# A new eight-visit order for the attention loop of a transformer block on one core

## The chip, the cores and the metric

The kernel runs on one core of a Trainium2 chip. The metric is device time in microseconds (us), from the first to the last instruction of the program, as the median of repeated runs. A core has five engines with a queue of their own each: TensorE (PE; its weight loads are listed as PEld), VectorE (DVE), ScalarE (ACT), GpSimd (POOL) and SyncE (SP, which here only issues DMAs). They meet at semaphores. Products of TensorE land in PSUM, eight banks of 128 x 512 fp32; VectorE or ScalarE read them from there, and a bank can be written again once its reader is done.

## The reference

One transformer block on a sequence of 2048 rows of width 448, all in fp32:

```
h   = x + softmax(q k^T / sqrt(28)) v wo      q = LN(x) wq (16 heads of 28), k, v = LN(x) wk, LN(x) wv (one head for all)
out = h + (silu(LN(h) w1) * (LN(h) w3)) w2    width 1792 inside
```

Softmax is taken over all 2048 keys. No mask.

## The kernel before, in words

**Stages.** Start (LN, queries, keys, values), attention, FFN. The change touches the attention loop.

**Blocks and visits.** Attention runs over 16 blocks `i`: four blocks of 512 query rows times four groups of four heads. Each block has 16 key chunks `c` of 128 keys. A pair (i, c) is a *visit*, 256 in all. A head takes 32 partitions, so that the four heads of a group lie in the four row groups of TensorE, and four products with 32 rows each can run there side by side.

**Head products (`H` in the order, class `Head`).** For each visit and head three products (high and low parts of keys and queries) add up the transposed scores of 128 keys by 512 queries in one bank; after the third ScalarE takes the exponential into a `pt` tile (or into the tiles `xh` and `xl`, which serve as the third buffer). So three `H` tokens of one head give one ScalarE instruction.

**Value products (`pv1`).** For a visit four products with 32 columns each, one per head, add values and the softmax denominator into the bank `po`. After a block's 16 visits ScalarE copies it out to `OT`. The token does nothing when a head of that visit isn't scored yet.

**Score-max units (class `Unit`).** To shift the exponentials, the row maximum of the scores is needed before a block's head products. It comes from separate products in the other orientation: 128 queries by 512 keys per unit, with four query blocks `n`, four key blocks `kt` and four heads, 64 units per block, done some 20 visits ahead. There are several kinds:

- `U`: one product, and VectorE reduces the bank to its maximum (`plain`, L333).
- `D` and `S`: a pair of key blocks a and b. `D` multiplies the query with the difference of the keys a - b (`KD`, made once at the start by GpSimd), and ScalarE evicts the positive part, Relu, to `ab` (L344). `S` multiplies with b, and one VectorE instruction adds `ab` and takes the maximum (L351). max(a, b) = b + Relu(a - b), so VectorE reduces two key blocks with one instruction.
- `E` and `R`: ScalarE copies a bank to the tile `kept` (L358), and VectorE reduces it later from there (L364).

When all 64 units of a block are counted (`counted`), `max_done` and `max_rows` reduce and transpose the maxima (L384, L389), and SP writes them as an extra row into the query tile by four small DMAs (L395).

**The order.** Attention's order is written out: a string `EVERY` of tokens, repeated until the last 20 visits. Before, a cycle has four `pv1`, 48 `H`, 11 `U`, and two `D`, two `S`, one `E` and one `R`. In it, heads 0 and 1 take the first two key blocks of every query block as a pair (`PAIRS`). The tail, a second list, has only head and value products. I call what lies between two value products a *stretch*. All engines run their queue in the order in which the tokens issue.

**Banks.** Seven of the eight banks serve heads and units; `po` has the eighth. `bank()` takes the free one that, by an own small model of the engines (class `Clock`), is free first. The model sets no order; it only decides which earlier eviction a product has to wait for.

Of the kernel before, what the change touches and what calls it, by code (L numbers as in the profile page):

```python
# [8 lines left out]
F32 = mybir.dt.float32  # L9
# [26 lines left out]
def block_kernel(  # L36
# [74 lines left out]
    class Clock:  # L111


        def __init__(self):
            self.mode, self.tile, self.started, self.loaded = None, {}, {}, {}
            self.load = self.start = self.end = self.drained = 0.0
            self.act = self.dve = 0.0

        def mm(self, mode, r, ps, us, first):
            if mode != self.mode:  # L120
                self.mode, self.tile, self.started, self.loaded = mode, {}, {}, {}
                self.drained = self.end + 0.095
            t = max(self.drained, self.load + 0.0035, self.started.get(r, 0.0) + 0.004, self.loaded.get(r, 0.0))
            if first:
                t = max(t, order[used[id(ps)][1]] + 0.017)
            self.load = t
            self.loaded[r] = t + (0.107 if mode != "pv" else 0.025)
            t = max(self.loaded[r], self.tile.get(r, 0.0), self.start + 0.0035)
            self.start = self.started[r] = t
            self.tile[r] = t + us  # L130
            self.end = max(self.end, t + us)
            ready[id(ps)] = t + us + 0.255

        def read(self, eng, t, every):
            t = max(getattr(self, eng), t)
            setattr(self, eng, t + every)
            return t

# [20 lines left out]
    def mm_D(ps0, ps, lhs, rhs, lsl, rsl, between=None, pairs_ab=((0, 0), (1, 0), (0, 1))):  # L159

        terms, rsl_n = [], rsl.stop - rsl.start
        for a, b in pairs_ab:
            terms += [(a, c, b, c) for c in range(3)]
        terms += [(0, 3, 0, 3), (0, 3, 1, 3)]
        for k, (a, ca, b, cb) in enumerate(terms):
            pe.matmul(  # L166
                ps, lhs[b][:, cb, lsl], (rhs[2] if ca == 3 and len(rhs) == 3 else rhs[a])[:, ca, rsl],
                start=(k == 0), stop=(k == len(terms) - 1),
            )
            clock.mm("full", 0, ps0, 0.0182 + rsl_n / 2400, k == 0)  # L170
            if between is not None and k == 5:
                between()
# [83 lines left out]
    def ln_tr_rows(t, n):  # L256
        if n == 0:
            TB.extend(bank() for c in range(4))
        for c in range(4):
            c0 = c * P if c < 3 else D - P  # L260
            pe.transpose(TB[c][:, n * P : (n + 1) * P], LN[t][3][n][:, c0 : c0 + P], ident)
            clock.mm("full", 0, TB[c], 0.109, n == 0)

    def ln_tr(t, c, spare=False):
        ps = last = TB[c] if TB else bank()
        if c == 0:
            XT[t] = xt_tiles()
        c0 = c * P if c < 3 else D - P
        xns = LN[t][3]
        for n in range(NQ):  # L270
            if TB:
                break
            pe.transpose(ps[:, n * P : (n + 1) * P], xns[n][:, c0 : c0 + P], ident)  # L273
            clock.mm("full", 0, ps, 0.109, n == 0)
        to_x(t, c, ps, last, spare)
# [37 lines left out]
    class Unit:  # L313
# [5 lines left out]
        def mm(self, keys=None):  # L319
            i, n, kt, r = self.i, self.n, self.kt, rows(self.j)  # L320
            MX[i] = MXT[i % 2]
            ps = bank("pa")
            pe.matmul(ps, QS[i][r, 0, n * P : (n + 1) * P], KS[0][r, kt * T : (kt + 1) * T] if keys is None else keys[r],  # L323
                      start=True, stop=True)
            clock.mm("rows", self.j, ps, 0.2293, True)
            return ps
# [4 lines left out]
        def red(self):  # L331
            ps = self.ps
            ve.tensor_reduce(self.to(), ps, axis=AX.X, op=ALU.max)  # L333
            done(ps, clock.read("dve", ready[id(ps)], 0.598) + 0.717)

# [4 lines left out]
        def diff(self):  # L340
            ps = self.mm(KDS[self.kt])
            self.ab = ab_pool[n_ab[0] % len(ab_pool)]
            n_ab[0] += 1
            se.activation(self.ab, ps, AF.Relu)  # L344
            t = clock.read("act", ready[id(ps)], 0.477)
            self.t = t + 0.634
            done(ps, t + 0.634)

        def sum(self):
            ps = self.mm(KS[0][:, (self.kt + 1) * T : (self.kt + 2) * T])  # L350
            ve.tensor_tensor_reduce(self.ab, ps, self.ab, 1.0, -3.0e38, ALU.add, ALU.max, self.to())  # L351
            done(ps, clock.read("dve", max(ready[id(ps)], self.t), 0.7) + 0.74)

        def copy(self):
            ps = self.mm()
            self.ab = kept[n_kept[0] % len(kept)]
            n_kept[0] += 1
            se.activation(self.ab, ps, AF.Copy)  # L358
            t = clock.read("act", ready[id(ps)], 0.477)
            self.t = t + 0.634  # L360
            done(ps, t + 0.634)

        def red_copy(self):
            ve.tensor_reduce(self.to(), self.ab, axis=AX.X, op=ALU.max)  # L364
            clock.read("dve", self.t, 0.575)

# [30 lines left out]
    class Head:  # L397
# [5 lines left out]
        def mm(self, k):  # L403
            i, c, r = self.i, self.c, rows(self.j)
            if k == 0:
                self.ps = bank()
            pe.matmul(self.ps, KS[k % 2][r, c * P : (c + 1) * P], QS[i][r, k // 2], start=(k == 0), stop=(k == 2))  # L407
            clock.mm("rows", self.j, self.ps, 0.2293, k == 0)

        def exp(self):  # L410
# [3 lines left out]
            se.activation(f(PT[i, c, p][:, jj]), self.ps, AF.Exp, bias=0.0, scale=SCALE)  # L414
            t = clock.read("act", ready[id(self.ps)], 0.477)
            PR[i, c] = max(PR.get((i, c), 0.0), t + 0.634)
            done(self.ps, t + 0.634)

    def pv(i, c):
        if c == 0:  # L420
            PO[i] = ps_o.tile([P, T], F32, name="po")
        for j in range(4):
            pe.matmul(PO[i][32 * j : 32 * j + 32], VA[:, c], f(PT[i, c, j // 2][:, j % 2]),  # L423
                      start=(c == 0), stop=(c == NC - 1))
        clock.load = max(clock.load, PR.pop((i, c)))
        clock.mm("pv", 0, PO[i], 0.868, False)
        if c == NC - 1:
            g = i % NG
            if i < NI - 2:
                se.activation(OT[:, g], PO.pop(i), AF.Copy)  # L430
            else:
                ve.tensor_copy(OT[:, g], PO.pop(i))
# [65 lines left out]

    PAIRS = (0, 1)
    KD = keep.tile([P, 2, T], F32R, name="KD", tag="q5")  # L500
# [374 lines left out]
    TAIL = LAST - AHEAD  # L875
    heads, left, tail = {}, [0] * 4, False
# [10 lines left out]
    open_d, waiting, later = {}, [], []  # L887
# [8 lines left out]
    kt_ = keep.tile([P, 2, T], F32, name="kept", tag="q4")  # L896
    kept, n_kept = [kt_[:, k] for k in range(2)], [0]

# [12 lines left out]
    def unit(kind, j):  # L911

        if kind == "S":
# [4 lines left out]
            return  # L918
        if kind == "R":
            if waiting:  # L920
                u = waiting.pop(0)
                u.red_copy()
                counted(u.i)
            return
        skip = 4 if kind == "E" else 0
        for k, (_, u, pair) in enumerate(todo_u[j]):
            if pair == (kind == "D"):
                if skip and k + 1 < len(todo_u[j]):
                    skip -= 1
                    continue  # L930
                todo_u[j].pop(k)
                if pair:
                    open_d[j] = u
                    u.diff()
                elif kind == "E":
                    waiting.append(u)
                    u.copy()
                else:
# [26 lines left out]
    while n_pv[0] + LAG < TAIL:  # L965
        for x in EVERY:
            tick()
            if x != "pv1":
# [13 lines left out]

    while waiting:
        unit("R", 0)
    tail = True
    homes, n_qs = [5, 6, 1, 2, 3, 4, 0], [0]
# [34 lines left out]
    def two(pairs):  # L1021
        for units in zip(*pairs):
            for h, (ps, lhs, rhs, first, last) in enumerate(units):
                pe.matmul(ps[:, : rhs.shape[-1]], lhs, rhs, start=bool(first), stop=bool(last), skip_group_check=True)  # L1024
                clock.mm("half", h, ps, 0.016 + rhs.shape[-1] / 2400, first)

# [175 lines left out]
```

## Time and profile before

| what | value |
|---|---|
| median of three runs | 1162.36 us (1159.97 to 1164.62) |
| span of the profiled execution | 1158.6 us |
| granted TensorE clock | 1.000 |
| PE busy | 1149.0 us (99%) |
| VectorE busy | 805.8 us (70%) |
| ScalarE busy | 764.3 us (66%) |
| GpSimd busy | 330.2 us (29%) |
| value products, first to last start | 89.3 to 738.6 us |
| busy within 89.3 to 738.6 us: PE, ScalarE, VectorE | 647.5, 613.7, 552.7 us |

The profile page is of one execution. Its execution has no time on record but its span; the timed runs are others. Busy time counts an engine as busy while any of its instructions is in flight, and instructions overlap in flight, so an engine that is busy all the time may still have room. Matmul ends are modelled. Three stretches of some 9 us within attention, at the end of every fourth block, belong to the output projection.

### The profile page before, as it was taken

The numbers are of one execution on the slowest core, as the hardware profiler recorded it, in microseconds if no ns is written. First come the engines' busy times: TensorE is split into PE (matmuls) and PEld (weight loads), VectorE is DVE, ScalarE is ACT, GpSimd is POOL, SyncE is SP. The second block draws the span as 40 slices with busy tenths as digits, with TensorE's granted clock in tenths as the row PEclk, the third lists the DMA queues.
The fourth block names the chain that finished last, engine by engine and source line by source line (L and its number), as shares of the span: only waits on it lengthen the run. The fifth ranks groups of instructions, "written<-read, shape, count | busy, mean of one in ns | idle before, by whom it ended". The sixth has DMA issues, their size and how long they took to land.

```text
span 1158.6 us, 25640 instructions
## 1 busy us (share of the span) xinstructions
PE 1149.0 (99%) x10154; PEld 772.7 (67%) x10154; DVE 805.8 (70%) x1498; ACT 764.3 (66%) x1587; POOL 330.2 (29%) x242
## 2 busy tenths in 40 slices
PE   8999999999999999999999999999999999999998
PEld 6664444446444445444445444589999999999997
DVE  8878999897999998999988983163543444344333
ACT  5649999997999997999997999512222222222221
POOL 5312001101101111110111011345565556556552
PEclk9999999999999999999999999999999999999999
DMA  4010100001000002000012100143211101000000
GB/s 168 10 38 1 34 13 18 19 15 47 19 12 10 19 24 54 19 20 3 19 24 55 50 19 14 56 103 96 73 39 20 41 1 49 17 33 33 1 1 33
DMA packets 66680, 38.15 MB, mean 33 GB/s; under 512 B 41728, under 2 KB 59392, under 8 KB 66560
## 3 DMA queue, kind: packets, MB, share of 16 engines
q1 hardware_dynamic: 66560, 36.51, 11.5%
q8 instruction: 79, 1.29, 0.5%
q14 instruction: 41, 0.34, 0.1%
HBM read 24.04 MB, written 7.47 MB: 27 GB/s over the span
## 4 chain that ended last, share of the span: by engine, by line
PE 94%; ACT 2%; DVE 2%; issue 1%; DMA 1%; SPq 0%; POOL 0%; ACTq 0%; POOLq 0%
PE po L423 21%; PE pb L407 20%; PE pa L1024 18%; PE pa L323 10%; PE pb L1024 9%; PE pa L166 5%; PE pb L166 4%; PE po L1024 4%; PE pb L1070 1%; ACT OT L430 1%; ACT ab L344 1%; DVE mx L333 1%; PE pb L273 0%; ACT pt L414 0%; PE po L166 0%
## 5 line engine op out<-in xcount | busy, mean ns | idle before, releaser
L333 DVE TENSOR_REDUCE mx<-pa 128x1 f32<-128x512 f32 x689 | 440.1, 685 | 22.1 <-PE pb L407 13.0
L407 PE MATMUL pb<-qs,KS 32*128 32x512 f32 x3072 | 384.9, 425 | 0.0
L414 ACT ACTIVATE pt<-pb 128x512 f32<-128x512 f32 x684 | 365.9, 621 | 20.1 <-PE pb L407 17.3
L407 PEld LDWEIGHTS pb<-qs,KS 32*128 32x128 f32 x3072 | 234.0, 182 | 132.2 <-ACT pt L414 66.9
L323 PE MATMUL pa<-KS,qs 32*128 32x512 f32 x886 | 311.7, 459 | 1.3
L1024 PE MATMUL pa<-xl,qs 64*128 64x512 f32 x1044 | 195.4, 388 | 0.0
L323 PEld LDWEIGHTS pa<-KS,qs 32*128 32x128 f32 x886 | 138.6, 182 | 83.6 <-DVE mx L333 46.3
L423 PE MATMUL po<-pt,VA 128*32 128x512 f32 x1368 | 182.2, 605 | 0.4 <-ACT pt L414 0.4
L1024 PE MATMUL pa<-xh,qs 64*128 64x512 f32 x739 | 159.9, 388 | 0.0
L454 POOL TENSOR_TENSOR OT<-OT,rb 128x512 f32<-128x512 f32 x15 | 19.7, 1311 | 458.1 <-DMA rb<-sd 240.9
L1024 PE MATMUL pb<-w2s,pt 64*128 64x448 f32 x1050 | 145.2, 360 | 0.0
L1034 DVE TENSOR_TENSOR pt<-pa,pt 128x512 f32<-128x512 f32 x49 | 33.8, 691 | 159.0 <-ACT pt L1032 152.9
L1024 PEld LDWEIGHTS pa<-xl,qs 64*128 64x128 f32 x1044 | 141.9, 184 | 3.1
L1024 PEld LDWEIGHTS pb<-w2s,pt 64*128 64x128 f32 x1050 | 125.2, 184 | 2.0 <-DVE pt L1040 0.2
L351 DVE CUSTOM_DVE_ANT_0 ab<-pa,ab 128x512 f32<-128x512 f32 x138 | 93.6, 686 | 39.5 <-PE pa L323 28.4
L1024 PEld LDWEIGHTS pa<-xh,qs 64*128 64x128 f32 x739 | 108.4, 184 | 3.2
L414 ACT ACTIVATE xl<-pb 128x512 f32<-128x512 f32 x170 | 99.6, 610 | 8.9 <-PE pb L407 6.8
L414 ACT ACTIVATE xh<-pb 128x512 f32<-128x512 f32 x170 | 104.5, 633 | 0.0
L1032 ACT ACTIVATE pt<-pa 128x512 f32<-128x512 f32 x49 | 29.3, 597 | 94.7 <-PE pa L1024 90.9
L423 PE MATMUL po<-xl,VA 128*32 128x512 f32 x340 | 89.4, 605 | 0.0
L423 PE MATMUL po<-xh,VA 128*32 128x512 f32 x340 | 89.4, 605 | 0.0
L344 ACT ACTIVATE ab<-pa 128x512 f32<-128x512 f32 x138 | 82.2, 608 | 6.7 <-PE pa L323 4.9
(156 smaller groups left out, 1411.4 us busy)
## 6 DMA issues: line engine op xcount, KB each, us to landing
rb<-sd SPq DMA_DIRECT2D x64, 64.0 KB
xr<-xn SPq DMA_DIRECT2D x64, 56.0 KB
QR<-OT SPq DMA_DIRECT2D x60, 56.0 KB
QR<-in_B_w_dram SPq DMA_DIRECT2D x16, 192.0 KB
xh<-xr SPq DMA_DIRECT2D x4, 768.0 KB
X<-in_A_x_dram SPq DMA_DIRECT2D x3, 896.0 KB
out_dram<-X SPq DMA_DIRECT2D x3, 896.0 KB
w<-in_B_w_dram SPq DMA_DIRECT2D x8, 192.0 KB
```

What stands on the lines that cost most here:

```text
L166: pe.matmul(ps, lhs[b][:, cb, lsl], (rhs[2] if ca == 3 and len(rhs) == 3 else rhs[a])[:, ca, rsl], start=(k == 0), stop=(k == len(terms) - 1),
L323: pe.matmul(ps, QS[i][r, 0, n * P : (n + 1) * P], KS[0][r, kt * T : (kt + 1) * T] if keys is None else keys[r], start=True, stop=True)
L333: ve.tensor_reduce(self.to(), ps, axis=AX.X, op=ALU.max)
L344: se.activation(self.ab, ps, AF.Relu)
L351: ve.tensor_tensor_reduce(self.ab, ps, self.ab, 1.0, -3.0e38, ALU.add, ALU.max, self.to())
L407: pe.matmul(self.ps, KS[k % 2][r, c * P : (c + 1) * P], QS[i][r, k // 2], start=(k == 0), stop=(k == 2))
L414: se.activation(f(PT[i, c, p][:, jj]), self.ps, AF.Exp, bias=0.0, scale=SCALE)
L423: pe.matmul(PO[i][32 * j : 32 * j + 32], VA[:, c], f(PT[i, c, j // 2][:, j % 2]), start=(c == 0), stop=(c == NC - 1))
L454: eng.tensor_tensor(o, o, rb, op=ALU.mult)
L1024: pe.matmul(ps[:, : rhs.shape[-1]], lhs, rhs, start=bool(first), stop=bool(last), skip_group_check=True)
L1032: se.activation(sg, ps[0], AF.Silu)
L1034: ve.tensor_tensor(sg, ps[1], sg, op=ALU.mult)
```

## The change

**The order.** `EVERY` becomes a cycle of eight visits: eight `pv1`, 96 `H`, 22 `U`, five `D` and five `S` tokens. `E`, `R` and their tile `kept` are gone. The loop now stops inside a cycle once the tail is due, and what units are left are then done at once.

**The pairs.** `PAIRS` holds (head, half of the key blocks, parity of the query block): per two query blocks, which are eight visits, head 0 has three pairs and head 1 has two, now also over key blocks 2 and 3. Their difference `KD2` is in both kernels made at the start; it keeps its buffer, which `kept` took over before.

**The tokens' code.** `unit` still keeps one open difference per head in `open_d`; it is not changed but for the loss of `E` and `R`. In the new list the `D` and `S` tokens stand in the order D0 D1 D1 S1 D0 S0 S0 S0 D0 S1. In the built programs:

| instructions | before | changed |
|---|---|---|
| Relu evictions of a difference (ScalarE) | 138 | 167 |
| copies to `kept` (ScalarE) | 59 | 0 |
| sums with maximum (VectorE) | 138 | 80 |
| plain reductions (VectorE) | 689 | 690 |
| reductions of `kept` (VectorE) | 59 | 0 |
| unit products (TensorE) | 1024 | 937 |
| row maxima finished, and transposed (VectorE) | 16 | 1 |
| DMAs of the maxima (SP) | 64 | 4 |

**The clock.** `Clock` gets other constants and rules (load times, read latencies, the value product as four products), which changes the choice of banks throughout.

```
+        LOAD = {"pv": 0.027, "tr": 0.08}
-        def mm(self, mode, r, ps, us, first):
+        def mm(self, mode, r, ps, us, first, after=0.0):
             if mode != self.mode:
-                self.mode, self.tile, self.started, self.loaded = mode, {}, {}, {}
-                self.drained = self.end + 0.095
-            t = max(self.drained, self.load + 0.0035, self.started.get(r, 0.0) + 0.004, self.loaded.get(r, 0.0))
+                self.mode, self.started, self.busy = mode, {}, {}
+                self.load = max(self.load, self.end - 0.075)
+            t = max(self.load + 0.0035, self.started.get(r, 0.0) + 0.002, after)
...
+        def act(self, t):
+            t = max(self.free["act"], t + 0.036, self.last - 0.27)
+            self.free["act"] = t + 0.4767
+            self.last = max(t + 0.592, self.last + 0.49)
+            return self.last
...
-    PAIRS = (0, 1)
+    PAIRS = ((0, 0, 0), (0, 0, 1), (0, 1, 0), (1, 0, 0), (1, 0, 1))
...
-            if j in PAIRS and kt < 2:
-                if kt == 0:
-                    todo_u[j].append((s // NQ, Unit(i, j, n, 0), True))
+            if (j, kt // 2, n % 2) in PAIRS:
+                if kt % 2 == 0:
+                    todo_u[j].append((s // NQ, Unit(i, j, n, kt), True))
...
-    EVERY = "U1 pv1 H3 D0 H1 U2 H3 H0 H1 H3 H0 H1 U2 U3 H0 pv1 D1 H2 S0 H3 H2 U3 H3 H2 H3 H1 H2 H2 H1 H1 U0 H2 H1 H0 H1 H0 U2 H1 H0 U3 pv1 R E3 H0 H2 H1 H0 H3 H2 H1 H3 H2 U0 H3 U2 H0 H1 pv1 H2 H0 S1 H3 H2 U1 H0 H3 H2 H3 H0".split()
+    EVERY = "pv1 D0 H3 H1 H2 H1 H3 H2 U0 H1 H3 U1 H2 U3 pv1 D1 H0 H2 U3 H2 H0 H3 H0 H2 H1 U3 H1 H1 H1 H1 H2 H3 H2 H0 H0 H3 U2 H0 H2 H1 U3 pv1 U2 H1 H0 H3 H3 H1 U2 H0 H3 H0 H1 U2 pv1 D1 H3 H0 H2 U1 H0 H2 H3 H3 H2 S1 H0 pv1 U2 H3 D0 H3 H0 H3 H0 H1 H1 U3 H2 H1 H2 H0 S0 H2 U1 S0 pv1 H1 S0 H3 H2 D0 H1 H3 H2 H0 H1 U2 H0 H3 U1 H2 H0 pv1 U2 H3 H2 H0 H3 H3 H1 H0 H3 H2 H0 H3 H1 H2 U0 H3 H1 U2 pv1 H1 H2 H0 U3 H2 H1 U3 S1 H0 H2 H1 U3 H0".split()
...
     while n_pv[0] + LAG < TAIL:
         for x in EVERY:
+            if n_pv[0] + LAG >= TAIL:
+                break
             tick()
...
-    while waiting:
-        unit("R", 0)
-    tail = True
+    for j in range(4):
+        unit("S", j)
+        while todo_u[j]:
+            for kind in ("DS" if todo_u[j][0][2] else "U"):
+                unit(kind, j)
+    while later:
+        tick()
```

**Where rows move.** First TensorE, in the middle of the loop. The rows go from one value product (`po`) to the next; `pb` are head products, `pa` unit products. Before, one of the two shorter stretches of a cycle:

```order
L423 MATMUL po<-pt,VA 32x512 x4
L323 MATMUL pa<-KS_85,qs 128x512
L407 MATMUL pb<-qs,KS_85 128x512 x3
L407 MATMUL pb<-qs,KS_86 128x512
L407 MATMUL pb<-qs,KS_85 128x512
L407 MATMUL pb<-qs,KS_86 128x512 x3
L407 MATMUL pb<-qs,KS_85 128x512
L323 MATMUL pa<-KS_85,qs 128x512
L407 MATMUL pb<-qs,KS_85 128x512
L323 MATMUL pa<-KS_85,qs 128x512
L407 MATMUL pb<-qs,KS_85 128x512 x2
L423 MATMUL po<-pt,VA 32x512 x4
```

In the changed program, the stretch that has the second `D1`:

```order
L419 MATMUL po<-xh,VA 32x512 x2
L419 MATMUL po<-xl,VA 32x512 x2
L333 MATMUL pa<-KD,qs 128x512
L403 MATMUL pb<-qs,KS_85 128x512 x3
L333 MATMUL pa<-KS_85,qs 128x512
L403 MATMUL pb<-qs,KS_86 128x512 x3
L403 MATMUL pb<-qs,KS_85 128x512 x2
L333 MATMUL pa<-KS_85,qs 128x512
L403 MATMUL pb<-qs,KS_85 128x512
L419 MATMUL po<-pt,VA 32x512 x4
```

Fifteen row products stood in the first, twelve stand in the second: a difference (`KD`), a plain unit, nine head products, and one sum.

Then VectorE, where the maxima of one block end and those of the next begin (`mx_97` and `mx_98` are the two buffers of maxima). Before:

```order
L333 TENSOR_REDUCE mx_97<-pa 128x1
L333 TENSOR_REDUCE mx_98<-pa 128x1 x3
L333 TENSOR_REDUCE mx_97<-pa 128x1
L384 TENSOR_REDUCE neg_82<-mx_97 128x16
L389 STREAM_TRANSPOSE mr<-neg_82 128x32
L351 ISA ab,mx_98<-pa,ab 128x512
L351 ISA mx_98 128x1
L333 TENSOR_REDUCE mx_98<-pa 128x1 x4
L364 TENSOR_REDUCE mx_98<-kept 128x1
```

In the changed program:

```order
L360 ISA ab,mx_97<-pa,ab 128x512
L360 ISA mx_97 128x1
L343 TENSOR_REDUCE mx_97<-pa 128x1 x4
L343 TENSOR_REDUCE mx_98<-pa 128x1
L343 TENSOR_REDUCE mx_97<-pa 128x1 x14
L442 RECIPROCAL sm<-sm 128x16
L343 TENSOR_REDUCE mx_97<-pa 128x1
```

The reduction over a block's maxima (`neg`) and its transpose (`mr`) no longer stand between two blocks, and the reductions form longer runs without a sum between them.

More of the change, by code (lines that the diff above doesn't have):

```diff
@@ L111, in block_kernel @@
     class Clock:
+        LOAD = {"pv": 0.027, "tr": 0.08}
         def __init__(self):
-            self.mode, self.tile, self.started, self.loaded = None, {}, {}, {}
-            self.load = self.start = self.end = self.drained = 0.0
-            self.act = self.dve = 0.0
-        def mm(self, mode, r, ps, us, first):
+            self.mode, self.started, self.busy = None, {}, {}
+            self.load = self.start = self.end = 0.0
+            self.free = {"act": 0.0, "dve": 0.0}
+            self.last = 0.0
@@ L124, in mm @@
             if first:
-                t = max(t, order[used[id(ps)][1]] + 0.017)
+                t = max(t, order[used[id(ps)][1]] + 0.052)
             self.load = t
[L127 to L137, printed above, removed]
+            self.start = t = max(t + self.LOAD.get(mode, 0.105), self.start + 0.0035,
+                                 self.started.get(r, 0.0) + self.busy.get(r, 0.0))
@@ new lines, in mm, with dve @@
+            if mode == "pv":
+                t += us
+            self.started[r], self.busy[r] = t, us
+            ready[id(ps)] = e = t + us + (0.138 if mode == "pv" else 0.158)
+            self.end = max(self.end, e)
+        def act(self, t):
[3 more added lines that the diff above has]
+            return self.last
+        def dve(self, t, every=0.598, lasts=0.685):
+            t = max(self.free["dve"], t + 0.037)
+            self.free["dve"] = t + every
+            return t + lasts
@@ L324, in mm @@
                       start=True, stop=True)
-            clock.mm("rows", self.j, ps, 0.2293, True)
+            clock.mm("rows", self.j, ps, 0.2267, True)
             return ps
@@ L351, in sum @@
             ve.tensor_tensor_reduce(self.ab, ps, self.ab, 1.0, -3.0e38, ALU.add, ALU.max, self.to())
[L352 to L365, printed above, removed]
+            done(ps, clock.dve(max(ready[id(ps)], self.t), 0.6, 0.7))
     def both(i, h, n, kt):
@@ L424, in pv @@
                       start=(c == 0), stop=(c == NC - 1))
-        clock.load = max(clock.load, PR.pop((i, c)))
-        clock.mm("pv", 0, PO[i], 0.868, False)
+        t = PR.pop((i, c)) + 0.051
+        for j in range(4):
+            clock.mm("pv", j, PO[i], 0.4533, False, t)
         if c == NC - 1:
@@ L875, in block_kernel @@
     TAIL = LAST - AHEAD
-    heads, left, tail = {}, [0] * 4, False
+    heads, left = {}, [0] * 4
     todo_u = [[], [], [], []]
@@ L1024, in two @@
                 pe.matmul(ps[:, : rhs.shape[-1]], lhs, rhs, start=bool(first), stop=bool(last), skip_group_check=True)
-                clock.mm("half", h, ps, 0.016 + rhs.shape[-1] / 2400, first)
+                clock.mm("half", h, ps, 0.0133 + rhs.shape[-1] / 2400, first)
     def settle(ps):
```

40 lines of the change are left out of this document (13 added, 27 removed).

## Prediction

> **What bounds the kernel now.** I read the windows first, by stage. The first two quoted windows are eight value visits of the attention loop each, the second of them with a block's end in it; the third is six visits of the tail, where score-max units have run out.
>
> ```profile
> core 0: us, PE busy (x) PEld busy (x) DVE busy (x) ACT busy (x) POOL busy (x), PEclk, DMA share, GB/s
> 296.70:316.30 19.60, 19.60 (x195) 9.51 (x193) 17.80 (x34) 19.29 (x39) 3.13 (x3) 1.00 0.11 27
> 316.30:336.30 20.00, 19.90 (x198) 9.17 (x196) 18.14 (x35) 19.67 (x41) 0.00 (x0) 1.00 0.01 2
> ...
> 711.70:723.70 12.00, 12.00 (x125) 4.79 (x124) 7.87 (x16) 11.96 (x25) 3.35 (x3) 1.00 0.11 30
> ```
>
> TensorE and ScalarE both look full, VectorE nearly so, and the granted clock is 1.00, so no clock effect is involved. Full twice over needs the next view: the chain of waits through one cycle of four visits (start, length, what). `po L423` is the value product, eight records a visit; `pb` and `pa` are head and unit products.
>
> ```profile
> 300.79 1.03 PE po L423 x8
> 301.82 0.42 PE pb L407
> ...
> 302.97 1.00 PE po L423 x8
> ...
> 306.52 1.04 PE po L423 x8
> 307.56 0.43 PE pa L323
> 307.98 0.46 PE pb L407 x8
> ...
> 308.69 0.99 PE po L423 x8
> ...
> 310.64 1.02 PE po L423 x8
> ```
>
> From 300.79 to 310.64 is 9.85 us; the next cycles repeat within 0.05, and two of them are the 19.6 of the window. I use 19.63 for eight visits. The four stretches last 2.18, 3.55, 2.17 and 1.95. On TensorE a stretch costs the value product (1.02), 0.43 until its first row product is through, and then 0.23 for each further *round*: four row products on the four heads' rows run together, and eight took 0.46. Thus TensorE needs 1.22 + 0.23 x rounds, where the rounds are the most products that any one head has in the stretch. Counted from the cycle's list, the stretches have 4, 7, 4 and 3 rounds: 2.14, 2.83, 2.14, 1.91, in all 9.02, or 18.04 per eight visits. Three stretches are at this floor. The long one is not: 3.55 against 2.83. What holds it stands in ScalarE's timeline and in the weight loads that wait within it:
>
> ```profile
> 302.45 0.20 PEld L323 LDWEIGHTS pa<-KS,qs 32*128 32x128 f32 x2 [0.17 <-DVE mx L333]
> 303.90 0.18 PEld L323 LDWEIGHTS pa<-KD,qs 32*128 32x128 f32 x1 [0.84 <-ACT pt L414]
> 305.08 0.18 PEld L323 LDWEIGHTS pa<-KS,qs 32*128 32x128 f32 x1 [0.19 <-ACT ab L344]
> ...
> 302.81 1.57 ACT L414 ACTIVATE pt<-pb 128x512 f32<-128x512 f32 x3
> 304.44 0.60 ACT L344 ACTIVATE ab<-pa 128x512 f32<-128x512 f32 x1
> 304.93 2.06 ACT L414 ACTIVATE pt<-pb 128x512 f32<-128x512 f32 x4
> 306.84 0.64 ACT L414 ACTIVATE xh<-pb 128x512 f32<-128x512 f32 x1
> 307.32 0.65 ACT L414 ACTIVATE pt<-pb 128x512 f32<-128x512 f32 x1
> 308.02 0.60 ACT L358 ACTIVATE kept<-pa 128x512 f32<-128x512 f32 x1
> ```
>
> Four exponentials take 2.06 though one lasts 0.62, so ScalarE starts one every 0.48 when it is fed. From 304.44 to 307.32 it runs at that pace: the long stretch is ScalarE catching up, and TensorE waits in it for the banks that ScalarE (0.19) and VectorE (0.17) still hold. (The 0.84 at 303.90 is the value product itself, which the load has to let pass; it recurs at every visit.) At 306.52 a value product starts; ScalarE has three instructions left, and its next one starts at 308.02, 0.70 after the one before it. Each visit thus costs it a few tenths: 38 instructions in eight visits are 38 x 0.48 = 18.24, and 19.63 - 18.24 = 1.39, or 0.17 per visit. ScalarE bounds the loop, with 0.17 per visit lost because banks and products reach it unevenly. VectorE has 28 reductions, at 0.62 each by the next row ((3.16 - 0.685) / 4), or 17.4: close behind.
>
> ```profile
> span 1158.6 us, 25640 instructions
> ...
> 301.12 3.16 DVE L333 TENSOR_REDUCE mx<-pa 128x1 f32<-128x512 f32 x5
> L333 DVE TENSOR_REDUCE mx<-pa 128x1 f32<-128x512 f32 x689 | 440.1, 685 | 22.1 <-PE pb L407 13.0
> ```
>
> Outside the loop (start to 89 us, FFN after 739 us) the order of the work is unchanged; only bank numbers can move. I cost that at 0, with 2 us either way.
>
> **The change, part by part.** It does not do all that its words say, and that decides the sum. The list opens differences in the order D0 D1 D1 S1 D0 S0 S0 S0 D0 S1, but `open_d` keeps one difference per head: a second D on the same head overwrites the first, and an S with nothing open does nothing. Of five differences per cycle two are summed. The built programs agree: Relu evictions go from 138 to 167, sums from 138 to 80, and 87 second products never happen. Since `counted` then never reaches zero, the row maximum is finished for the first block alone, and exponentials of later blocks run with a shift of zero; exactly, softmax is the same under any shift.
>
> ```profile
> L344 ACT ACTIVATE ab<-pa 128x512 f32<-128x512 f32 x138 | 82.2, 608 | 6.7 <-PE pa L323 4.9
> L351 DVE CUSTOM_DVE_ANT_0 ab<-pa,ab 128x512 f32<-128x512 f32 x138 | 93.6, 686 | 39.5 <-PE pa L323 28.4
> ...
> L358 ACT ACTIVATE kept<-pa x59: 597/597/600, 90.9 to 692.8; 128x512 f32<-128x512 f32 x59
> ...
> L384 DVE TENSOR_REDUCE neg<-mx x16: 219/220/221, 78.1 to 697.1; 128x16 fp32r<-128x64 f32 x16
> ...
> L395 SPq DMA_DIRECT2D qs<-mr x64: 520/543/659, 78.6 to 699.4; - x64
> ```
>
> Per eight visits:
>
> - *ScalarE.* 32 exponentials stay; two copies and four Relus become five Relus: 38 to 37 instructions, 18.24 to 17.76, a gain of 0.48.
> - *VectorE.* 22 plain reductions stay; four sums and two reductions of the copy become two sums: 28 to 24, 17.4 to 14.9. This lies beside ScalarE and is worth nothing alone, but VectorE gives banks back sooner.
> - *TensorE.* 128 row products become 125. The new stretches have 3, 3, 5, 4, 6, 3, 4 and 7 rounds, 35 against 36: floor 8 x 1.22 + 35 x 0.23 = 17.81, from 18.04.
> - *Maximum, its transpose and four small DMAs per block.* 0.22 us of VectorE and 0.54 of SP's queue for each DMA, both idle enough; I cost their removal at nothing. Head products of a block no longer depend on that DMA. No term for it: the window with a block's end is 0.4 longer than the other, and the eviction of a block's outputs, which ScalarE has there besides (0.48), accounts for that.
> - *The second pair's keys* are already made at the start; they keep the buffer that the copies had. No new instruction.
>
> Order of evictions: ScalarE is now given 3, 4, 5, 5, 5, 3, 4 and 8 instructions in the eight stretches, before 5, 3, 4 and 7, twice. Taking for each stretch the larger of TensorE's floor and 0.48 x its ScalarE instructions gives before 2 x (2.40 + 1.91 + 2.14 + 3.36) = 19.62, which is the measured 19.63. The same rule gives now 1.91 + 1.92 + 2.40 + 2.40 + 2.60 + 1.91 + 2.14 + 3.84 = 19.12: 0.51 less. This is the lower bound of the gain if bank choice gives nothing. The upper end: the tail, where ScalarE (4 x 0.48 = 1.92) and TensorE (1.22 + 3 x 0.23 = 1.91) are matched and VectorE has hardly any work, takes 12.00 / 6 = 2.00 per visit, 4% over its floor; 1.04 x 17.81 = 18.5, or 1.1 less.
>
> The bank clock does not add an instruction; it decides which bank a product waits for. The wait counts in the built programs allow ScalarE on average 4.5 unfinished instructions as a value product starts, 4.3 before, and 5, not 4, at the one that ends the long stretch. One more there is worth up to 0.48. I take about half of it on top of 0.51: 0.78 per eight visits, 18.85.
>
> One rule makes another sum of this. The Trainium skill, Perfetto Trace Analysis, section Identifying the Most-Contended Engine, takes ScalarE's occupancy as a fair measure of how near it is to its limit: by it 19.29 of 19.60 leaves nothing but the instruction less, 19.63 x 37 / 38 = 19.11. The trace disagrees in part, as its rows overlap (four in 2.06 that last 0.62 each).
>
> The mixed stretch has some 234 visits, 29 cycles of eight: 29 x 0.78 = 22.6 us. The tail keeps its order and cost. The profiled execution's own span is 1158.6 us; the timed runs are 1159.97 to 1164.62, so their median lies 3.8 above it. What is saved in the loop is the same in both: 1162.4 - 22.6 = 1140.
>
> **The rivals.**
>
> - *ScalarE has its one instruction less and nothing else* (0.48 to 0.51 per cycle, 14 to 15 us): 1148. For it: the larger-of rule fits the cycle before to 0.01. Against it: the deeper backlog and VectorE's 2.5 us of slack.
> - *The loop balances as in the tail* (18.1 to 18.6, 30 to 44 us): 1126. For it: two engines matched there at 4% loss. Against it: the new stretches are uneven (3 to 8 ScalarE instructions).
> - *TensorE sets the end*, as the chain reads if it is taken by its names (PE almost throughout): only one round less, 0.23 x 29 = 6.7 us, 1156. Against it: its floor of 18.04 is 1.6 short of the cycle, and its loads wait for banks.
> - *Slower: ScalarE runs dry before the long stretch.* The three stretches before it give ScalarE 12 instructions, 5.76, in at least 6.65 of TensorE's time. If the two value products there find one instruction less in hand than now, each loses 0.48: 17.76 + 1.39 + 0.96 = 20.11, 29 x 0.48 = 14 us more, 1176. It decides from 0.23 lost per visit ((19.63 - 17.76) / 8) against 0.17 now. Against it: before, the same sum over the two stretches ahead of the long one (7 instructions, 3.36, in 4.05) did no such harm.
>
> **How the numbers follow.** Forecast 0.44 (1132 to 1146), ScalarE alone 0.20, balanced 0.22, TensorE 0.08, dry 0.06. A measurement here cannot tell less than about 0.5%, 5.8 us, from no change. Faster: 0.44 + 0.20 + 0.22 = 0.86; the same 0.08 (the TensorE case lies on its edge); slower 0.06. The range takes in the first two cases and most of the third, with 2 us for the rest of the program: 1119 to 1155.
>
> **What would show it.** In the changed profile: 167 Relus beside 80 sums; no row maximum after the first block; 37 ScalarE starts per eight visits and a cycle near 18.85, of which the long stretch takes about 3.5; VectorE's share of the loop down by a seventh; the tail still at 2.0 a visit. I am wrong if the cycle is above 19.4 or below 18.2, if the gain lies outside the loop, or if ScalarE's starts are more than 0.2 per visit short of 0.48 apart.

## The result and the profile after

The changed kernel takes 1146.35 us (four runs, 1145.83 to 1147.00), the kernel before 1161.25: a ratio of 0.9871, 95% interval 0.9854 to 0.9888, or 15 us less. The forecast was 22.6 us less.

All of it lies in the stage in which heads and units are mixed. Windows by stage, first of the kernel before, then of the changed one (columns as in the prediction): start, mixed loop of 232 visits, tail, FFN.

```profile
0.00:89.30 89.30, 85.17 (x448) 60.90 (x448) 72.87 (x172) 49.71 (x90) 30.49 (x44) 1.00 0.21 70
89.30:691.30 602.00, 600.66 (x5703) 295.85 (x5701) 538.38 (x1013) 567.98 (x1122) 72.16 (x74) 1.00 0.10 24
691.30:737.30 46.00, 45.55 (x448) 17.93 (x449) 13.97 (x28) 45.05 (x91) 9.92 (x7) 1.00 0.05 13
737.30:1158.60 421.30, 417.61 (x3565) 397.99 (x3564) 180.55 (x287) 101.57 (x289) 217.63 (x118) 1.00 0.15 40
```

```profile
0.00:89.10 89.10, 84.75 (x449) 60.55 (x449) 71.79 (x170) 49.69 (x90) 30.04 (x43) 1.00 0.21 70
89.10:677.20 588.10, 588.10 (x5620) 298.12 (x5618) 466.87 (x811) 552.03 (x1092) 72.67 (x75) 1.00 0.10 24
677.20:723.10 45.90, 45.90 (x450) 17.52 (x449) 14.18 (x28) 44.43 (x89) 9.89 (x7) 1.00 0.05 13
723.10:1144.20 421.10, 417.42 (x3557) 397.32 (x3556) 180.72 (x287) 101.81 (x289) 217.57 (x118) 1.00 0.15 41
```

The loop goes from 602.0 to 588.1, 13.9 less; the other stages differ by 0.2 at most. VectorE loses 71 us of work there, ScalarE 16. Eight visits without and with a block's end, then the chain of value products through one cycle of the changed kernel:

```profile
291.50:310.65 19.15, 19.15 (x194) 9.48 (x194) 15.54 (x28) 18.79 (x38) 3.12 (x3) 1.00 0.10 28
310.65:330.10 19.45, 19.45 (x190) 9.39 (x189) 15.38 (x27) 19.01 (x39) 0.00 (x0) 1.00 0.01 1
```

```profile
291.47 1.06 PE po L419 x8
...
293.47 1.03 PE po L419 x8
...
295.43 1.00 PE po L419 x8
...
298.10 1.02 PE po L419 x8
...
300.27 0.99 PE po L419 x8
...
302.97 0.99 PE po L419 x8
...
304.89 1.04 PE po L419 x8
...
307.06 0.99 PE po L419 x8
```

Of the 29 cycles half have no block's end and go from 19.64 to 19.18, half have one and go from 19.97 to 19.47: 14.5 x (0.46 + 0.50) = 13.9. Differences (Relu), sums and finished maxima are as counted in the built programs:

```profile
L354 ACT ACTIVATE ab<-pa x167: 590/599/677, 36.4 to 675.1; 128x512 f32<-128x512 f32 x167
L360 DVE CUSTOM_DVE_ANT_0 ab<-pa,ab x80: 678/682/692, 39.7 to 682.5; 128x512 f32<-128x512 f32 x80
...
L380 DVE TENSOR_REDUCE neg<-mx x1: 219/219/219, 78.0 to 78.0; 128x16 fp32r<-128x64 f32 x1
```

What a cycle is made of shows by the stretches from one value product to the next, as medians over the loop of the starts in each trace (us; visits without a block's end):

| kernel | stretches of eight visits | sum |
|---|---|---|
| before | 2.13 1.95 2.16 **3.58** 2.13 1.95 2.16 **3.58** | 19.64 |
| changed | 1.96 1.94 2.70 2.15 2.70 1.93 2.17 **3.63** | 19.18 |

The long stretch is as long as ever, but there is one per eight visits where there were two; what stood in the other now makes two stretches of 2.70.

### The profile page after: what moved, and what is told of

It reads as the page before. It is cut to its first block, busy times and chain, and to the rows that moved or that the text cites. A ratio compares the mean times of both kernels' runs of the same rounds, so it can differ in the third digit from the quotient of the medians.

```text
span 1144.2 us, 25235 instructions
## 1 busy us (share of the span) xinstructions
PE 1136.2 (99%) x10067; PEld 773.5 (68%) x10067; DVE 733.6 (64%) x1294; ACT 748.0 (65%) x1557; POOL 330.2 (29%) x242
## 4 chain that ended last, share of the span: by engine, by line
PE 97%; DVE 1%; issue 0%; ACT 0%; DMA 0%; POOL 0%; DVEq 0%; POOLq 0%
PE po L419 23%; PE pb L403 19%; PE pa L1012 18%; PE pa L333 13%; PE pb L1012 9%; PE pa L176 5%; PE po L1012 4%; PE pb L176 4%; PE pb L1058 1%; PE pb L283 0%; PE po L176 0%; DMA X<-in_A_x_dram 0%; ACT ab L354 0%; DVE X L1080 0%; DVE xn L223 0%
## 5 line engine op out<-in xcount | busy, mean ns | idle before, releaser
L343 DVE TENSOR_REDUCE mx<-pa 128x1 f32<-128x512 f32 x690 | 446.2, 686 | 117.4 <-PE pb L403 62.8
L410 ACT ACTIVATE pt<-pb 128x512 f32<-128x512 f32 x684 | 361.0, 620 | 21.0 <-PE pb L403 9.5
L403 PE MATMUL pb<-qs,KS 32*128 32x512 f32 x3072 | 364.1, 430 | 0.0
L403 PEld LDWEIGHTS pb<-qs,KS 32*128 32x128 f32 x3072 | 230.4, 182 | 80.9 <-ACT pt L410 32.1
L333 PE MATMUL pa<-KS,qs 32*128 32x512 f32 x770 | 260.0, 451 | 0.0
L333 PEld LDWEIGHTS pa<-KS,qs 32*128 32x128 f32 x770 | 122.0, 181 | 95.5 <-ACT pt L410 48.6
L354 ACT ACTIVATE ab<-pa 128x512 f32<-128x512 f32 x167 | 99.5, 606 | 10.5 <-PE pa L333 8.9
L1020 ACT ACTIVATE pt<-pa 128x512 f32<-128x512 f32 x49 | 29.4, 599 | 94.7 <-PE pa L1012 90.6
L481 POOL TENSOR_TENSOR qs<-QR,qs 128x1024 fp32r<-128x1024 f32 x32 | 76.6, 2394 | 18.7 <-DVE qs L480 18.7
```

The lines of the kernel that those rows point to most:

```text
L481: ge.tensor_tensor(wl, W13[k], f(wh), op=ALU.subtract)
L1020: se.activation(sg, ps[0], AF.Silu)
```

## The experiments

Three causes were open: the bank clock, the sums and maxima that are left out, and the list itself with its one ScalarE instruction less. Against my theory that ScalarE's count sets the cycle (0.48 us each and 1.4 of waits) stood a rival that I had not costed in the prediction: row products issue in the list's order, so that one whose head is still busy holds up all behind it. Replaying each stretch by that rule alone (0.23 per product on the same head) gives a floor of 18.97 for the cycle before and 18.77 for the changed one, where the prediction's count of rounds gave 18.04 and 17.81. The expectations below call this rule TensorE's order. The trace contradicts it, as the last section shows. Each ratio is to the kernel before in the same series of runs, whose median lies between 1160.48 and 1160.77 us.

**The bank clock alone, taken away and given.** The class `Clock`, its constants and its calls go back to those of before, in the changed list (e1); a second kernel (e2) has the opposite, the old list with the new class.

```
-                self.load = max(self.load, self.end - 0.075)
+                self.drained = self.end + 0.095
...
-            self.free["act"] = t + 0.4767
+            self.t_act = t + 0.477
...
-            clock.mm("pv", j, PO[i], 0.4533, False, t)
+        clock.mm("pv", 0, PO[i], 0.868, False)
```

> The changed kernel's order with the bank clock of the kernel before (its class, constants and read calls); the work is the same as in the changed kernel, which sums two of five differences and finishes the maximum for the first block alone. If the bank clock brought the gain: a cycle of eight visits back near 19.6 us and 1160 us. If the order and the work left out brought it: 19.2 us and within 3 us of 1146. In between, the difference is the clock's share.

> The kernel before (its order, all its sums and maxima) with the new bank clock. If the clock brought the gain: a cycle of eight visits near 19.2 us and 1147 us. If it brought none: 19.63 us and within 3 us of 1161.

Measured: the changed list with the old clock 1147.17 us, ratio to the kernel before 0.9880 (0.9864 to 0.9897), cycle 19.19; the old list with the new clock 1160.35, ratio 1.0000 (0.9991 to 1.0010), cycle 19.61. The clock is worth 0.03 per cycle at most in either list, which is nothing against the 0.46 of the change.

**The left-out work alone (e3).** The list of before without its two sum tokens: the differences are still made, but never summed, so that the sums and the maxima after the first block are left out.

```
-  EVERY = "... D1 H2 S0 H3 ... H2 H0 S1 H3 ..."
+  EVERY = "... D1 H2 H3 ... H2 H0 H3 ..."
```

> The kernel before with S0 and S1 taken out of its list: no difference is summed in the loop, so four unit products and four VectorE instructions fewer per eight visits and, as in the changed kernel, no maximum after the first block. ScalarE's 38 instructions stay. ScalarE theory (cycle = 0.48 x its instructions + 1.4): 19.6 us, no change, 1161 us. If the left-out sums and maxima brought the gain: 19.2 us or less and 1147 us or less. TensorE's order (row products issue in the list's order, and one that waits for its head's row group holds up those behind it, by 0.23 us): that floor goes from 18.97 to 18.95, so no change.

Measured: 1160.18 us, ratio 0.9995 (0.9985 to 1.0004).

```profile
297.08:316.70 19.62, 19.62 (x189) 8.98 (x188) 15.51 (x26) 19.30 (x40) 3.12 (x3) 1.00 0.10 28
```

VectorE has 15.5 us of work where it had 17.8, the same relief as in the changed kernel, and the cycle stays at 19.62. In the list of before, sums and maxima cost nothing.

**The changed list with all its sums (e4).** A queue of open differences per head, so that none is overwritten, and a buffer for them.

```
-    open_d, later = {}, []
+    open_d, later = {j: [] for j in range(4)}, []
+    ab2 = keep.tile([P, 2, T], F32, name="ab2", tag="q4")
+    ab_free = ab_pool + [ab2[:, k] for k in range(2)]
...
-            if j in open_d:
-                u = open_d.pop(j)
+            if open_d[j]:
+                u = open_d[j].pop(0)
```

> The changed kernel with every difference summed: open differences are kept per head in a queue, with four buffers instead of two, so that all five S tokens of a cycle act, and the maxima of all blocks are finished and written. Against the changed kernel: three unit products and three VectorE instructions more per eight visits, ScalarE's 37 unchanged, the maximum's work back. ScalarE theory: 19.2 us, 1147 us. TensorE's order: its floor goes from 18.77 to 19.44, so 19.85 us and 1166 us, slower than the kernel before. If lost work made the gain: 19.6 us or more, 1160 us.

Measured: 1204.79 us, ratio 1.0379 (1.0363 to 1.0394): 58 us more than the changed kernel. Lost work (1160 or more) is the reading that holds, and both other numbers (1147 and 1166) fall short. The cycle is 20.75, or 22.21 with a block's end. In one place the three sums of head 0 stand close together on VectorE, with one plain reduction behind the first, and TensorE waits for their banks (VectorE's timeline, then a weight load):

```profile
360.99 0.68 DVE L360 CUSTOM_DVE_ANT_0 ab<-pa,ab 128x512 f32<-128x512 f32 x1
...
362.19 0.68 DVE L360 CUSTOM_DVE_ANT_0 ab<-pa,ab 128x512 f32<-128x512 f32 x1
...
362.88 0.69 DVE L360 CUSTOM_DVE_ANT_0 ab<-pa,ab 128x512 f32<-128x512 f32 x1
...
363.63 0.18 PEld L333 LDWEIGHTS pa<-KS,qs 32*128 32x128 f32 x1 [0.51 <-DVE mx L360]
```

And the maximum of a block can come too late. Here its four DMAs are issued from 388.60 on, over 2.71 us, and the first head product of the next block waits for them until 392.50 (SP's timeline, then TensorE's):

```profile
388.60 2.71 SPq L391 DMA_DIRECT2D qs<-mr  x4
...
392.50 0.50 PE L403 MATMUL pb<-qs,KS 32*128 32x512 f32 x3 [1.10 <-DMA qs<-mr]
```

Behind eight of the 15 such writes from the second on a weight load of a head product stands idle for 1.0 to 1.4 us, 9 us in all; most of the 58 us is the longer cycle. So the changed list has no room for the work that it names: what it gains depends on three of five sums, and the maxima, being left out.

**Fewer and more ScalarE instructions, and one more row product.** Three kernels, from the changed one: in e5 a `Y` token takes its pair off the list without computing it (in place of the three differences that are never summed); in e8 the Relu of the difference at the head of the long stretch is issued twice; in e9 the first product of head 1 in the long stretch is.

```
-    EVERY = "pv1 D0 H3 ... pv1 D1 H0 H2 U3 ... S0 H3 H2 D0 H1 ..."
+    EVERY = "pv1 Y0 H3 ... pv1 Y1 H0 H2 U3 ... S0 H3 H2 Y0 H1 ..."
...
             se.activation(self.ab, ps, AF.Relu)
+            if twice:
+                se.activation(self.ab, ps, AF.Relu)
...
+        if twice and k == 0:
+            heads[j].mm(3)
         heads[j].mm(k)
```

> The changed kernel without the three differences per cycle that are never summed: their product and Relu are left out, the two that are summed stay, the maximum is finished for the first block alone as in the changed kernel. ScalarE goes from 37 to 34 instructions per eight visits, row products from 125 to 122. ScalarE theory: 34 x 0.48 + 1.4 = 17.7 us, 43 us less, 1104 us. TensorE's order: its floor stays at 18.77, so at best 18.8 to 19.0 us, 5 to 11 us less, 1135 to 1141.

> The changed kernel with one more ScalarE instruction per eight visits: the difference at the head of the long stretch is evicted twice. ScalarE theory: 0.48 per cycle more, 19.65 us, 14 us slower, 1160. TensorE's order: no more than a few hundredths, 1146 to 1148.

> The changed kernel with one more row product per eight visits, on head 1 in the long stretch, where that head's products stand behind each other (a head's first product issued twice). TensorE's order: 0.23 per cycle more, 19.4 us, 6.7 us slower, 1153. ScalarE theory: nothing, since the long stretch is the one where ScalarE catches up.

Measured: three instructions fewer 1139.05 us, ratio 0.9814 (0.9771 to 0.9856); one more 1163.97, ratio 1.0025 (1.0011 to 1.0038); one more row product 1148.84, ratio 0.9898 (0.9855 to 0.9941). In cycles: 19.10, 19.73 and 19.29. ScalarE's count by itself does not price the first two: three fewer should have given 1.44 and gave 0.08, except at a block's end, where the output eviction that cost 0.3 is now hidden (19.10 there too, from 19.47). The 1139 lies in the range that TensorE's order gave (1135 to 1141), but not for its reason: most of the gain lies at the blocks' ends. One more cost 0.55, more than its own 0.48, where TensorE's order allowed a few hundredths. The row product cost 0.11, which is neither the 0.23 of TensorE's order nor nothing. The long stretch of the kernel with one more (ScalarE's timeline, then a late weight load; the value product before it starts at 313.65):

```profile
315.18 0.60 ACT L354 ACTIVATE ab<-pa 128x512 f32<-128x512 f32 x1
315.81 0.60 ACT L357 ACTIVATE ab<-pa 128x512 f32<-128x512 f32 x1
316.30 0.59 ACT L413 ACTIVATE pt<-pb 128x512 f32<-128x512 f32 x1
316.78 0.60 ACT L413 ACTIVATE xl<-pb 128x512 f32<-128x512 f32 x1
...
317.43 0.18 PEld L333 LDWEIGHTS pa<-KS,qs 32*128 32x128 f32 x1 [0.20 <-ACT xl L413]
```

The second eviction at 315.81 pushes the stretch's first exponential to 316.30, 2.65 after the value product; every later one, and the banks that the last row products wait for, follow at 0.48. The second eviction starts 0.63 after the first, not 0.48; the two write the same tile. The stretch grows from 3.63 to 4.21. Without any difference there, ScalarE simply waits for that exponential (the value product starts at 304.81):

```profile
304.74 1.58 ACT L410 ACTIVATE pt<-pb 128x512 f32<-128x512 f32 x3 [0.44 <-PE pb L403]
306.80 0.60 ACT L410 ACTIVATE pt<-pb 128x512 f32<-128x512 f32 x1 [0.48 <-PE pb L403]
307.30 0.59 ACT L410 ACTIVATE xl<-pb 128x512 f32<-128x512 f32 x1
...
307.94 0.18 PEld L333 LDWEIGHTS pa<-KS,qs 32*128 32x128 f32 x1
```

306.80 is 1.99 after the value product, and the stretch takes 3.60. The second exponential ends at 307.89, and 0.05 later the load of the stretch's last unit product starts (307.94), as it does in the kernel with one more (317.38, then 317.43). The long stretch is thus a chain: value product, the three products of the first head, its exponential about 2.0 after the start, then the second exponential at ScalarE's pace, and last the unit product that needs its bank. An instruction taken out ahead of that exponential saves nothing, one that is put there delays it.

**Two instructions per eight visits taken from ScalarE elsewhere.** In the list of before, the token `X3` takes the unit that was copied off the list without computing it (e7).

```
-  EVERY = "... pv1 R E3 H0 H2 ..."
+  EVERY = "... pv1 X3 H0 H2 ..."
```

> The kernel before without its copied unit: product, copy on ScalarE and reduction of one unit in sixteen are left out, and so is the maximum after the first block. ScalarE goes from 38 to 36 instructions per eight visits, but none of the two is in the long stretches. ScalarE theory by the cycle (0.48 x instructions + 1.4): 18.7 us, 28 us less, 1133. Two limits by the stretch (each lasts the larger of its row products in the list's order and of ScalarE's instructions at 0.48, less what ScalarE has in hand): the long stretches keep 7 instructions and 3.58 us, the others are at TensorE's order already; 19.5 to 19.6 us, 1157 to 1161.

Measured: 1160.49 us, ratio 1.0003 (0.9993 to 1.0014), cycle 19.62.

```profile
296.74:316.39 19.65, 19.65 (x192) 9.50 (x191) 16.64 (x32) 18.31 (x38) 3.12 (x3) 1.00 0.10 27
```

ScalarE's busy time falls from 19.29 to 18.31 and the cycle does not move. This ends the theory that ScalarE's count sets the cycle; the two limits by the stretch (19.5 to 19.6) came out right.

**The order within the stretches.** Each stretch keeps its tokens, but the heads alternate (e6); the second kernel (e12) also leaves out the three differences that are never summed.

```
-  EVERY = "... pv1 D1 H0 H2 U3 H2 H0 H3 H0 H2 H1 U3 H1 H1 H1 H1 ..."
+  EVERY = "... pv1 D1 H2 H0 U3 H1 H2 H0 H3 H1 H2 H0 U3 H1 H2 H0 ..."
```

> The changed kernel's tokens with the same content in every stretch, but within a stretch the row products of the four heads alternate; the work is the changed kernel's. TensorE's order: the floor of a cycle falls from 18.77 to 17.74, and with 0.4 of waits the cycle is 18.2 us, 1118 us. ScalarE theory: its 37 instructions stand, 19.2 us and 1146 us, or more, as the heads now finish in bunches.

> The changed kernel without the three differences that are never summed, and with the heads alternating within each stretch: both limits of the long stretch are lowered at once (row products in order from 3.53 to 2.81, ScalarE from 8 to 7 instructions, 3.36). Two limits by the stretch: the long stretch falls from 3.63 to about 3.3, the cycle from 19.2 to 18.7 to 18.8, 1130 to 1134, although alternating alone made it longer. If alternating itself does harm (heads that finish in bunches): 19.1 us or more, 1139 or more.

Measured: 1152.73 us, ratio 0.9932 (0.9903 to 0.9960), cycle 19.41; both together 1142.78, ratio 0.9844 (0.9824 to 0.9863), cycle 19.19. The forecasts by TensorE's order (1118, and 1130 to 1134 for both) failed; what holds is the other reading of each expectation, that alternating does harm (1146 or more, and 1139 or more). Alternating heads takes 1.0 off the floor by order and still costs 0.23 in the cycle and 0.09 beside e5. The long stretch of the second kernel (value product at 305.51):

```profile
305.43 1.58 ACT L410 ACTIVATE pt<-pb 128x512 f32<-128x512 f32 x3 [0.39 <-PE pb L403]
307.56 0.60 ACT L410 ACTIVATE xl<-pb 128x512 f32<-128x512 f32 x1 [0.55 <-PE pb L403]
308.05 0.59 ACT L410 ACTIVATE pt<-pb 128x512 f32<-128x512 f32 x1
...
307.85 0.18 PEld L403 LDWEIGHTS pb<-qs,KS 32*128 32x128 f32 x2 [0.59 <-DVE mx L343]
...
308.69 0.18 PEld L333 LDWEIGHTS pa<-KS,qs 32*128 32x128 f32 x1
```

The first exponential comes at 307.56, 2.05 after the value product, as before; until 307.85 TensorE has no bank to go on with. The second exponential ends at 308.64, and 0.05 later the load of the last unit product starts (308.69). The chain is the same as in e5, and the order of the heads does not shorten it.

**No units.** No unit is computed. The loop has the tail's list of 48 head and four value products (e10) or, in a second kernel, an even list (e11).

```
-    open_d, later = {}, []
+    open_d, later, todo_u = {}, [], [[], [], [], []]
...
-    EVERY = "pv1 D0 H3 H1 ..."
+    EVERY = "H2 H0 H2 H1 H3 H0 H2 H1 H0 H3 H2 H0 H3 H1 H2 pv1 H2 H0 H1 ..."
...
+    EVERY = "H0 H1 H2 H3 H0 H1 H2 H3 H0 H1 H2 H3 pv1 ..."
```

> The changed kernel without any score-max unit in the loop: the tail's list of head and value products throughout. The maximum of the first block alone is made, at the start, and exponentials of the other blocks run without a shift, as in the changed kernel. TensorE's order: the list's floor is 16.16 us per eight visits, so 16.1, as the tail took in the kernel before, and 88 to 90 us less, 1057 to 1060. ScalarE theory (32 x 0.48 + 1.4): 16.8 us, 1077.

> As the kernel without units, but each visit has its twelve head products in turn over the heads (H0 H1 H2 H3, three times) before its value product: TensorE's floor is 8 x 1.91 = 15.3 us per eight visits, ScalarE's 15.4. Two limits: 15.4 to 15.8 us, 1047 to 1055. If bunched heads do harm: 16.2 us or more, 1060 or more.

Measured: with the tail's list 1076.85 us, ratio 0.9276 (0.9262 to 0.9290), faster than both kernels; with the even list 1558.36, ratio 1.3423 (1.3401 to 1.3445).

```profile
271.74 0.99 PE po L419 x8
273.63 0.99 PE po L419 x8
275.53 1.00 PE po L419 x8
...
277.41 1.06 PE po L419 x8
...
279.83 0.99 PE po L419 x8
```

The first runs at the pace of its row products: stretches of 1.89, 1.90, 1.88 and 2.42 where the replay says 1.91, 1.91, 1.90 and 2.36 (the count of rounds gives the same within 0.01), and eight visits in 16.24 against 16.16. ScalarE's count would have made it 16.8; that its total, 1077, was met is luck. The total is above the forecast of 1057 to 1060 for another reason: the last 15 stretches take 39.3 us, in the changed kernel 29.4, since the list is started anew there and the heads lose their lead over the value products, which wait some 8 us for exponentials there; the first three stretches take 12.0, where three at the loop's pace would take 6. The even list shows what no lead costs. Each value product follows its own visit's heads at once and waits for their exponentials (what waited for what, over eight visits: us in all, times, longest):

```profile
PEld po L419 <- ACT pt L410: 11.1, 20, 1.2
ACT pt L410 <- PE pb L403: 10.4, 5, 2.1
```

Every visit takes 4.15. That is a fault in my list, and it says nothing on bunched heads.

## Why the prediction was right, and where it was wrong

- **The sign and the place** held, and the time lies in the range: 14 us in the loop where 22.6 were forecast, nothing outside, the tail at 2.0 a visit, 167 Relus beside 80 sums, one maximum.
- **The step that was mis-sized is the bank clock.** I had put about 0.27 per cycle on a deeper queue for ScalarE, 29 x 0.27 = 7.8 us; the clock measured 0.03 or less per cycle in both lists (e1, e2). Without it the sum is 0.51 x 29 = 14.8 us, where 15 were measured; that it fits so well is luck, as the larger-of rule below shows. Why the room that the wait counts allow brings nothing is not shown.
- **"ScalarE bounds the loop, with 0.17 per visit lost" is wrong as a price by the count.** Two instructions fewer in the list of before changed nothing (e7), three fewer in the changed list 0.08 per cycle (e5), one more cost 0.55 (e8). It bounds one stretch, after that stretch's first exponential. The forecast of ScalarE's instruction less and nothing else (1148), a rival, came within 2 us of the time; e7 shows that this agreement was chance, since there ScalarE's busy time falls by 1 us per cycle and the time by nothing. The Trainium skill, Perfetto Trace Analysis, section Identifying the Most-Contended Engine, takes ScalarE's occupancy as a fair measure of how near it is to its limit: the same run speaks against it here, 19.29 to 18.31 of busy time in a cycle that stays at 19.6.
- **The larger-of rule** gave 19.12 and 19.18 was measured, but by errors that cancel: I had 2.40 for a stretch that takes 2.70, 2.40 for one that takes 2.15, 2.60 for the other of 2.70, and 3.84 for one that takes 3.63. What it left out are the waits for banks: in the two stretches of 2.70 the last load that waits for a bank starts 0.04 after VectorE gives that bank back (2.28 and 2.27 after the value product, in 58 of 59 such stretches). The prediction's reading that TensorE waits in the long stretch for banks of ScalarE and VectorE held; the rule of the list's order, which comes close with 2.61 and 2.59, does not.
- **"VectorE's relief is worth nothing alone"** held exactly (e3). **The cost of the maximum at nothing** held for the list of before (e3), but not for the changed one with all its sums, where the late write held some next blocks up by 1.0 to 1.4 (e4).
- **The tail as a model of balance** was a misreading. I took three rounds for each of its stretches; its list has 3, 3, 3 and 5 in four visits, which gives 4 x 1.22 + 14 x 0.23 = 8.10, or 2.02 a visit. Its 2.00 is TensorE's own time, with no loss of 4% on top.

What made the gain, then: not the clock (e1, e2); not the left-out sums and maxima by themselves (e3); not fewer ScalarE instructions by count (e7, e5). What remains is the list, which has one long stretch in eight visits instead of two, and which has room for two sums, not five (e4). The left-out work is needed for the gain all the same, since with it the changed list is slower than the kernel before (e4). That the number of long stretches is the cause is read from the stretch table; no run changed that number alone. What makes a long stretch long is the chain from the value product over two exponentials to the last unit product: in the kernel before, the changed one, e5, e6, e8, e9 and e12 the load of that product starts 0.04 to 0.06 after ScalarE gives its bank back. This is why alternating heads gains nothing there.

## What to carry to other kernels

Price a stage that has several engines near their limits by its stretches between two fixed points, with the chain of banks in each, and not by an engine's count over the cycle: an instruction costs what it delays in its own stretch, from nothing to more than its duration. Before costing a list or a planner's order, run its tokens through the code that reads them; here that showed that three of five differences were opened for nothing, and the run that repairs it is 44 us slower than the kernel before. If a result is no longer used, as the maxima after the first block, take out all that makes it: that is worth 70 us beyond this change (e10). The changed kernel and e10 run their exponentials without a shift after the first block; no run here tried scores too large for that.

## What the runs showed of the hardware that I had not expected

**Loads wait for banks where no wait is listed.** The end of the changed kernel's long stretch (weight loads, then VectorE, then ScalarE):

```profile
309.96 0.18 PEld L333 LDWEIGHTS pa<-KS,qs 32*128 32x128 f32 x1
...
310.14 0.18 PEld L333 LDWEIGHTS pa<-KS,qs 32*128 32x128 f32 x1
...
306.67 3.23 DVE L343 TENSOR_REDUCE mx<-pa 128x1 f32<-128x512 f32 x5 [0.26 <-PE pb L403]
...
309.49 0.60 ACT L410 ACTIVATE xl<-pb 128x512 f32<-128x512 f32 x1
```

But for the first, which lets the value product pass (0.84), none of the stretch's 26 loads is listed with a wait, since other loads are in flight meanwhile. Yet 309.96 comes 0.06 after the last of the five reductions (306.67 + 3.23 = 309.90), and 310.14 comes 0.05 after the second exponential (309.49 + 0.60 = 310.09). By the times of the semaphores in the trace, seven of the 26 loads start 0.04 to 0.06 after ScalarE or VectorE gives a bank back, in each of the 15 long stretches without a block's end.

**A busy head does not hold up the row products behind it.** I had taken the opposite for a rule, and engines were said above to run their queue in the order of the tokens; TensorE's row products do not keep to it. This is the stretch of the kernel before whose program order stands first under "Where rows move": a unit, nine head products, a unit, one head product, a unit, two head products. They start like this:

```profile
307.49 0.50 PE L323 MATMUL pa<-KS,qs 32*128 32x512 f32 x1
307.49 0.95 PE L407 MATMUL pb<-qs,KS 32*128 32x512 f32 x8
...
308.06 0.38 PE L323 MATMUL pa<-KS,qs 32*128 32x512 f32 x1
308.06 0.62 PE L407 MATMUL pb<-qs,KS 32*128 32x512 f32 x4
...
308.29 0.39 PE L323 MATMUL pa<-KS,qs 32*128 32x512 f32 x1
```

The second unit is ahead of the ninth head product, and two head products are ahead of the third unit. Here this is a matter of nanoseconds. In the first stretch of 2.70 of the changed kernel it is 0.17 us: the fourth product to start, 1.17 after the value product, can only be head 1's first, the eighth of the list, since heads 0, 2 and 3 had each started one 0.17 earlier, and products of one head are 0.23 or more apart. The four that stand before it in the list, on heads 0 and 3, start at 1.34 and 1.57.
